# Tiles of rows j and j+3 of one batch, numerator products over 128 rows, and a new written order, in a linear attention kernel with a mixture of adapters behind it

## The chip, the core and the metric

The kernel runs on one core of a Trainium2 chip. The metric is the time of the device for one execution, in microseconds (us). One execution of the kernel before was also taken by the hardware profiler; its rows are what the profile shows. Engines: TensorE (PE in the profile, PEld for its weight loads), VectorE (DVE), ScalarE (ACT), GpSimd (POOL), SyncE (SP, which issues every DMA here, one queue, in program order).

## The reference

Two parts, one behind the other. For each of 8 batches and 8 heads, with 576 rows of 64 columns:

```python
theta = np.pi / 2.0 * pos / S
def phi(x, c, s):
    r = np.maximum(x, 0.0)
    return np.concatenate([r * c, r * s], axis=-1)
q_p, k_p = phi(q, cos_w, sin_w), phi(k, cos_w, sin_w)
kv  = np.einsum('bhsf,bhsd->bhfd', k_p, v)
z   = np.sum(k_p, axis=2)
num = np.einsum('bhsf,bhfd->bhsd', q_p, kv)
den = np.einsum('bhsf,bhf->bhs', q_p, z)[..., None] + 1e-06
x   = num / den                      # then laid out as (8*576, 8*64)
logits = x @ w_gate                  # 8 experts, the best 2 kept, softmax weights w
out = x + sum over the 2 of  w * (x @ A[e]) @ B[e]        # rank 16
```

Inputs q, k and v are 28.3 MB in float32, the output is 9.4 MB.

## The kernel before

Rows of a batch are laid out as row 9p+j, with p in 0..63 and j in 0..8: half a partition axis holds the 64 values of p. Two heads share the partitions on loading (`load`, L381: `"b (g hp) (p j) d -> (hp p) (b g) (j d)"`), so a load has 128 partitions. K and Q come in units: batches 0 to 3 alone (1.18 MB each), batches 4 and 5 together and 6 and 7 together (2.36 MB each). V comes by batch.

Work on a unit, by the names that the written order uses:

- `LK0`, `LV0`, `LQ0`: a load. `st8.0`: store 0 of the group of tiles that ends with tile 8.
- `cK0.1`, `cQ0.1` (`e_cast`, L429): a pass over three values of j, 768 columns for a single batch or 1536 for two, float32 to bfloat16. For K it is also the relu (ScalarE at L436 or VectorE at L438); for Q it is a cast alone (L301, L303, L305), the relu of Q comes later.
- `phiK0.4`, `phiQ0.4` (`e_phi`): the second half of the features, the first half times tan (L309 on ScalarE, L312 on VectorE and GpSimd), 256 or 512 columns. `vs0.4`: V times cos into the `vb` tile, with the same two lines.
- `kv0.1` (L496): 24 products that add up K'V of a batch; `ke0` copies the result out of PSUM.
- `tq7` (L603): 8 transposes that bring a tile's Q features onto the partitions. `eq6` (L620, L622): copies two tiles out of PSUM, with Q's relu, into a `qt` tile.
- `nd7` (`e_nd`, L637): numerators and denominators of a tile. A tile is 128 rows in two halves of 64. For each of 8 heads and each half there is one product with 64 stationary columns (L645), which writes the half's 64 partitions of PSUM, and four more products add the epsilon (L652).
- `rd6`, `nx6` (L671, L676): reciprocal and multiplication, two tiles together, into an `x` tile.
- `tx7`, `ex6` (L696): transposes of x and their copy. `za7` (L721): products with the adapters' A and the gate. `mx`, `nt`, `d`, `ge`, `sg`, `w`, `zg`: the choice of two experts and their weights, for a group of tiles. `tz`, `ez` (L782): transpose of the weighted z and its copy. `dx7` (L806, L808): x plus the adapters' product. `eo6`: copy of the output of one or two tiles into an `o` tile (six of them; three lie in the first K buffer, once K4 has been read).

There are 36 tiles in groups. For batches 0 to 3 a tile pairs rows j and j+5 of one batch (j in 0..3), and row 4 is paired with that of another batch; batches 4 to 7 pair the same row of two batches. Groups are of two or three tiles, and one at the end: 15 groups.

Nothing decides the order at run time. The string `ORDER` lists every operation with its engine (`=V` VectorE, `=S` ScalarE, `=G` GpSimd) and its buffer (`@2`), and `replay` (L127) emits them in that order. Each engine takes its own instructions strictly in the listed order, and waits for what the instruction reads and for its buffer. `fill=14@0` stands for 14 matmuls of no use to the result (L832). SP's order of loads is `LQ0 LK0 LV0 LQ1 LV1 LK1 LK2 LQ2 LV2 ldw LQ3 LK3 LV3 LK4 LV4 LV5 LQ4 LK6 LV7 LV6`, two stores (`st1.0 st1.1`), `LQ6`, and then the other stores.

Of the kernel before, what the change touches and what calls it, by code (L numbers as in the profile page):

```python
# [72 lines left out]
LK3@3 phiQ0.8=G kv0.2 cQ1.2=G@3 tq3 ke0=S@0 cQ1.0=S@5 nd0@2 cQ1.1=G@4 nd1 fill=7@6 phiQ1.2=S
phiQ1.0=V phiQ1.5=G eq2=S@1 LV3@0 vs1.0=V@1 phiQ1.8=G rd0@1 vs1.4=G nx0@1 phiQ1.6=G sig vs1.7=G
tq4@4 phiQ1.1=G nd2@0 vs1.8=G tx0@6 cK1.0=V@2 phiQ1.7=S nd3 vs1.5=G cK1.1=V@3 tx1 fill=7@7
phiK1.2=S vs1.6=G vs1.2=S cK1.2=V@4 phiK1.5=G rd2@0 LK4@0 phiK1.7=S phiK1.3=G nx2@0 vs1.1=S
phiQ1.3=G cK2.2=S@1 vs1.3=G phiK1.4=V tq6@0 phiK1.1=G cK2.1=S@0 LV4@1 phiK1.8=V tq5 phiK1.0=V
eq4=S@1 phiQ1.4=V kv1.0@2 phiK1.6=V cK2.0=V@5 kv1.1 kv1.2 phiK2.6=V cQ2.0=G@0 tq7 ke1=V@3
ex0=S@1 tx2@7 tx3 cQ2.1=G@2 phiK2.1=V nd4@2 nd5 fill=6@6 phiQ2.2=S phiK2.7=G phiK2.5=V
phiK2.0=S rd4@0 phiK2.2=S nx4@2 vs2.0=G@2 phiQ2.0=S vs2.1=G vs2.2=S phiK2.4=V vs2.7=G vs2.4=S  # L80
eq6=V@1 kv2.0@2 vs2.5=S phiQ2.5=G tq8@4 phiQ2.1=S vs2.3=G tq9 aw phiK2.8=S phiK2.3=G tx4@6 tx5
vs2.6=S vs2.8=G ex2=V@0 za0@0 cQ2.2=S@5 LV5@2 kv2.1 eq8=V@0 kv2.2 LQ4@0 za2@1 cQ3.2=G@3 ke2=S@1
za1 za3 mx2@0 ex4=S@1 mx0@1 nd8@2 mx1 phiQ3.6=G mx3 nd9 fill=8@7 ge1 nt1=V nt3=G ge3 phiQ2.8=G
d1 phiQ2.7=V sg1 cQ3.1=G@4 cQ3.0=S@1 d3 rd8@2 w1=V phiQ2.3=S nx8@3 phiQ3.1=G cK3.0=S@1 zg1
cK3.1=S@0 nd6@2 phiK3.1=G phiQ3.7=V nd7 phiK3.0=G phiQ3.2=V tz1@0 sg3 tq12@6 w3=G ez1=S@1 rd6@1
phiK3.2=G nx6@4 phiQ3.0=S za4@0 za5 vs3.0=G@0 cK3.2=S@2 vs3.2=G mx4@2 tq14@4 vs3.7=S mx5 LK6@2
phiK3.6=G phiQ3.5=V dx0@2 nt5=V phiK3.7=S phiK3.8=G d5 dx1 zg3 vs3.8=G ge5 eo0=S@0 tx8@1
phiK3.3=V tq15 vs3.5=V vs3.4=G eq14=V@1 vs3.1=S tz3@3 tq13 phiK3.5=G vs3.3=S tx6@2 vs3.6=G tx7
ez3=S@0 phiK3.4=V kv3.0@4 phiQ2.6=G eq12=V@0 sg5 ex6=S@0 kv3.1 phiQ2.4=G kv3.2 phiQ3.3=G tx9
w5=V ke3=S@0 dx2@2 zg5 ex8=V@1 cK4.0=S@2 tz5@0 nd14@4 nd15 ez5=V@1 dx4@0 rd14@1 nx14@1 dx5  # L90
phiK4.1=G dx3 eo4=S@1 phiQ3.8=G eo2=V@2 tq10@4 phiK4.2=G tq11 cK4.1=S@4 za9@6 tx14@0 eq10=V@1
tx15 za6@7 za7 phiK4.5=G za8 ex14=S@1 mx6@0 nd10@2 mx7 cK4.2=V@0 nd11 fill=7@1 phiK4.0=S rd10@2
mx8 vs4.0=S@1,2 vs4.7=G nt8=V vs4.8=S vs4.2=G nx10@2 phiK4.7=S vs4.5=G vs4.1=V tx10@5 phiQ3.4=S
d8 kv5.0@0 mx9@1 sg8 phiK4.3=V vs4.6=S vs4.4=G tx11 ge8 phiK4.8=V tq16@2 phiK4.6=S vs4.3=G tq17
ex10=V@0 phiK4.4=G eq16=S@1 LV7@1 w8=V za10 kv4.0@4 LV6@0 mx10 kv4.1 zg8 nt10=G cQ4.1=G@2 kv5.1
st1.0 cQ4.0=V@0 kv4.2 tz8@7 st1.1 ke4=S@3 kv5.2 cQ4.2=G@4 LQ6@2 nd12@2 nd13 st5.1 d10 ez8=V@1
sg10 ke5=S@2 ge10 rd12@0 nx12@0 phiQ4.1=S dx6@0 phiQ4.3=G dx7 phiQ4.0=G dx8@7 w10=V eo6=S@3
phiQ4.4=G zg10 eo8=V phiQ4.5=S tz10@7 st8.0 cK6.1=S@2 nd16@2 ez10=V@0 nd17 cK6.0=V@0 tq18@0
za15@6 cK6.2=S@4 rd16@0 tq19 nx16@4 za11@7 eq18=S@0 phiK6.8=G phiQ4.2=V tx16@2 tx17 mx15@1
tq20@4 ex16=V@0 phiK6.6=G tq21 mx11@2 tx12@3 phiQ4.6=G eq20=V@1 za16 tx13 za17 dx9@0 ex12=S@0  # L100
dx10 mx16 mx17 ge17 nt17=G eo9=S@4 phiK6.2=G za12 d17 nd18@2 mx12 nt12=V nd19 phiK6.7=G d12
sg17 st10.0 ge12 tq22@0 sg12 rd18@1 vs6.0=G@0,1 nx18@3 tq23 st3.1 w12=G eq22=S@0 st10.1 w17=G
phiK6.3=G zg12 nd20@2 zg17 tz12@7 phiK6.0=G nd21 ez12=V@0 dx11@6 vs6.8=S rd20@2 phiQ4.7=G
tz17@0 nx20@2 dx12 vs6.2=G ez17=S@1 za13@1 za14 eo11=S@5 tx18@0 vs6.3=G mx13@0 dx15@2 mx14 ge14
tq24@4 nt14=V phiK6.4=G d14 vs6.1=V tq25 sg14 vs6.5=S cQ6.0=G@0 dx16 eq24=V@1 tx20@6 eo15=S@0
tx21 dx17@7 tx19 w14=V vs6.4=G zg14 nd22@2 ex18=S@1 ex20=V@0 nd23 vs6.7=G tz14@1 rd22@0
ez14=S@0 phiQ6.2=G nx22@4 eo17=S dx13@0 dx14 phiK6.5=V nd24@2 eo13=S@4 phiK6.1=V nd25 phiQ4.8=V
kv6.0@6 vs6.6=V phiQ6.0=S st14.1 kv6.1 rd24@0 nx24@0 za18@1 cQ6.2=S@2 st17.0 za19 kv6.2 st12.1
# [759 lines left out]
```

## Time and profile before

| | us |
|---|---|
| median of 3 runs | 124.34 (124.27 to 124.65) |
| profiled execution | 124.38 |
| its span, first to last instruction | 122.6 |
| TensorE busy | 98.9 (81% of the span) |
| VectorE busy | 88.6 (72%) |
| ScalarE busy | 87.4 (71%) |
| GpSimd busy | 61.4 (50%) |

DMA moved 38.59 MB. "Busy" counts the time of instructions, with their pipeline latency: single matmuls are given with 0.2 to 0.4 us where the next one starts 0.02 to 0.2 us later, so a step's cost on TensorE is read from the distance of starts, or from the chain of waits, which counts each stretch once. A row of the timeline gives start, duration, engine, line, operation, output and input; in brackets stand the idle time ahead of it and what ended that.

### The profile page before, as it was taken

The numbers are of one execution on the slowest core, as the hardware profiler recorded it, in microseconds if no ns is written. First come the engines' busy times: TensorE is split into PE (matmuls) and PEld (weight loads), VectorE is DVE, ScalarE is ACT, GpSimd is POOL, SyncE is SP. The second block draws the span as 40 slices with busy tenths as digits, with TensorE's granted clock in tenths as the row PEclk, the third lists the DMA queues.
The fourth block names the chain that finished last, engine by engine and source line by source line (L and its number), as shares of the span: only waits on it lengthen the run. The fifth ranks groups of instructions, "written<-read, shape, count | busy, mean of one in ns | idle before, by whom it ended". The sixth has DMA issues, their size and how long they took to land.

```text
span 122.6 us, 4766 instructions
## 1 busy us (share of the span) xinstructions
PE 98.9 (81%) x2048; PEld 71.9 (59%) x2048; DVE 88.6 (72%) x225; ACT 87.4 (71%) x130; POOL 61.4 (50%) x114
## 2 busy tenths in 40 slices
PE   4969795859698889998875697999998979999720
PEld 1334563457484768676745567776897866874300
DVE  1008625597988888999496879899689978878700
ACT  5049489389967996989865996897984685767720
POOL 3045999366659696539497189846390010011000
PEclk9999999999999999999999999999999999999997
DMA  2999999999999999999999999960698100997992
GB/s 56 404 396 392 390 396 388 392 388 351 349 393 391 391 387 386 390 389 388 388 390 388 392 405 406 398 274 21 170 233 246 55 0 15 397 274 269 349 410 94
DMA packets 16532, 38.59 MB, mean 315 GB/s; under 512 B 1920, under 2 KB 1920, under 8 KB 16512
## 3 DMA queue, kind: packets, MB, share of 16 engines
q1 hardware_dynamic: 16512, 38.29, 86.4%
q8 instruction: 16, 0.26, 1.0%
q14 instruction: 4, 0.03, 0.1%
HBM read 28.85 MB, written 9.44 MB: 312 GB/s over the span
## 4 chain that ended last, share of the span: by engine, by line
DMA 42%; PE 21%; DVE 17%; SPq 11%; issue 2%; ACT 1%; POOL 0%; DVEq 0%
DMA k<-in_k_dram 28%; DMA v<-in_v_dram 14%; SPq L384 11%; DVE x L676 7%; PE psum L603 5%; PE psum L721 4%; PE psum L696 3%; PE psum L645 3%; PE psum L808 2%; PE psum L806 2%; DVE qt L622 2%; DVE zg L766 1%; DVE rd L671 1%; PE psum L782 1%; ACT xt L301 1%
## 5 line engine op out<-in xcount | busy, mean ns | idle before, releaser
L603 PE MATMUL psum<-ident,qp 128*128 128x128 bf16 x288 | 20.3, 219 | 5.7 <-DVE x L676 3.7
L676 DVE TENSOR_TENSOR x<-psum,rd 128x1024 bf16<-128x1024 f32 (+1 forms) x19 | 22.2, 1168 | 0.7
L603 PEld LDWEIGHTS <-qp 128*128 128x128 bf16 x288 | 17.0, 98 | 8.6 <-issue 4.7
L312 POOL TENSOR_SCALAR kp<-kp,tanw 128x256 bf16<-128x256 bf16 (+1 forms) x24 | 14.3, 601 | 11.6 <-ACT kp L436 9.5
L312 POOL TENSOR_SCALAR vb<-v,cosw 128x256 bf16<-128x256 f32 (+1 forms) x32 | 17.8, 567 | 3.9 <-DMA v<-in_v_dram 3.8
L303 POOL CAST qp<-q 128x768 bf16<-128x768 f32 (+1 forms) x11 | 12.2, 1125 | 14.8 <-DMA q<-in_q_dram 9.0
L832 PE MATMUL psum<-ident 128*128 128x512 bf16 x68 | 17.6, 409 | 1.9 <-POOL ident masks.py:199 1.8
L645 PE MATMUL psum<-kv,qt 128*64 128x65 bf16 x576 | 14.1, 197 | 2.8 <-DVE x L676 2.6
L645 PEld LDWEIGHTS <-qt 128*64 128x64 bf16 x576 | 12.4, 111 | 6.0 <-issue 3.6
L620 ACT ACTIVATE qt<-psum 128x2048 bf16<-128x2048 bf16 (+1 forms) x8 | 14.1, 1758 | 2.5 <-PE psum L603 1.6
L312 POOL TENSOR_SCALAR qp<-qp,tanw 128x256 bf16<-128x256 bf16 (+1 forms) x26 | 14.5, 564 | 0.3
L806 PE MATMUL psum<-x,ident 128*128 128x512 bf16 x36 | 13.7, 379 | 0.7 <-ACT kv L301 0.6
L436 ACT ACTIVATE kp<-k 128x768 bf16<-128x768 f32 (+1 forms) x10 | 10.7, 1094 | 5.0 <-DMA k<-in_k_dram 5.0
L622 DVE TENSOR_SCALAR qt<-psum 128x2048 bf16<-128x2048 bf16 (+1 forms) x11 | 12.9, 1170 | 1.8 <-PE psum L603 1.5
L808 PE MATMUL psum<-Bb,zt 128*128 128x512 bf16 x36 | 13.7, 379 | 0.1
L696 PE MATMUL psum<-ident,x 128*128 128x128 bf16 x144 | 12.4, 221 | 1.5 <-DVE x L676 1.5
L721 PE MATMUL psum<-AW,xt 128*128 128x136 bf16 x144 | 12.7, 223 | 1.2 <-DVE xt L305 0.3
L496 PE MATMUL psum<-vb,kp 64*128 64x65 bf16 x576 | 11.5, 190 | 1.2 <-POOL vb L312 1.1
L832 PEld LDWEIGHTS <-ident 128*128 128x128 bf16 x68 | 6.6, 104 | 9.7 <-issue 2.2
L696 PEld LDWEIGHTS <-x 128*128 128x128 bf16 x144 | 9.6, 114 | 4.0 <-DVE x L676 2.7
L438 DVE TENSOR_SCALAR kp<-k 128x768 bf16<-128x768 f32 (+1 forms) x8 | 5.0, 654 | 9.4 <-DMA k<-in_k_dram 9.4
L496 PEld LDWEIGHTS <-kp 64*128 64x128 bf16 x576 | 9.8, 94 | 3.1 <-issue 1.1
(56 smaller groups left out, 166.6 us busy)
## 6 DMA issues: line engine op xcount, KB each, us to landing
v<-in_v_dram SPq DMA_DIRECT2D x8, 1152.0 KB, 15.2
q<-in_q_dram SPq DMA_DIRECT2D x4, 1152.0 KB, 10.5
k<-in_k_dram SPq DMA_DIRECT2D x4, 1152.0 KB, 13.6
k<-in_k_dram SPq DMA_DIRECT2D x2, 2304.0 KB, 18.8
q<-in_q_dram SPq DMA_DIRECT2D x2, 2304.0 KB, 17.8
out_dram<-k SPq DMA_DIRECT2D x10, 256.0 KB, 5.1
out_dram<-o SPq DMA_DIRECT2D x9, 256.0 KB, 5.5
out_dram<-o SPq DMA_DIRECT2D x3, 768.0 KB, 5.1
```

Source lines behind the costliest of these rows:

```text
L312: eng.tensor_scalar(out=o_ap, in0=i_ap, scalar1=by, scalar2=0.0, op0=ALU.mult, op1=ALU.add)
L496: nc.tensor.matmul(out=psum[:, s + hp, h2 * W:(h2 + 1) * W], lhsT=kp[hp * 64:hp * 64 + 64, bi * H2 + h2, :], rhs=vb_t[hp * 64:hp * 64 + 64 ...
L603: nc.tensor.transpose(out=o_ap[:, hi, h2, :], in_=qv[:, bi * H2 + h2, :], identity=ident)
L620: nc.scalar.activation(o_ap, i_ap, AF.Relu)
L622: nc.vector.tensor_scalar(out=o_ap, in0=i_ap, scalar1=0.0, scalar2=None, op0=ALU.max)
L645: nc.tensor.matmul(out=psum[hi * 64:hi * 64 + 64, s + g, x * W:(x + 1) * W], lhsT=qt[:, qi, hi, h2, hp * 64:hp * 64 + 64], rhs=kv_t[KV[b][ ...
L676: nc.vector.tensor_tensor(out=x_t[Y["x"].slot][:, 0:n].rearrange("p n (g i d) -> p (n g) i d", g=2, i=4), in0=f()[:, :, :, 0:D], in1=r().t ...
L696: nc.tensor.transpose(out=bank16(s, 1024)[:, i * 512 + c * 128:i * 512 + (c + 1) * 128], in_=xv[:, c, :], identity=ident)
L721: nc.tensor.matmul(out=psum[:, s, i * ZW:(i + 1) * ZW], lhsT=xt_t[Z["xt"].slot][:, zi, c, :], rhs=AW[:, c, :], start=(c == 0 and i == 0), ...
L806: nc.tensor.matmul(out=psum[:, s, :], lhsT=ident, rhs=x_t[Y["x"].slot][:, yi, :], start=True, stop=False)
L808: nc.tensor.matmul(out=psum[:, s, :], lhsT=zt_t[Gd["zt"].slot][:, i, :], rhs=Bb, start=False, stop=True)
L832: nc.tensor.matmul(out=psum[:, s, :], lhsT=ident, rhs=warm, start=True, stop=True, skip_group_check=True)
```

## The change

1. Tiles. For every batch, tiles 0 to 2 of it hold rows j and j+3 of that batch (j = 0, 1, 2; stored as two stores of 64 partitions with three rows each), and rows 6 to 8 are paired with those of the other batch of a pair. 24 of 36 tiles are then of one batch. All groups have three tiles, but the last two (two and one): 13 groups instead of 15, 21 stores instead of 25.
2. In a tile of one batch both halves multiply the same K'V, so one product with 128 stationary columns does both: 8 products and 2 for the epsilon instead of 16 and 4. `qt` is laid out so that a head's two halves lie side by side, which changes where `tq` writes in PSUM, and not its count. A small tile `epsx` holds the epsilon of both halves.
3. The relu pass of K may run on GpSimd too, as a `tensor_scalar` with max, float32 to bfloat16. The new order puts 7 of the 18 there (five of 768 columns, two of 1536), 7 on ScalarE and 4 on VectorE; before it was 10 and 8.
4. `ORDER` is a new one: other order, engines and buffers throughout. Loads: `LK0 LQ0 LK1 LV0 LV1 LQ1 LK2 ldw LV2 LQ2 LK3 LQ3 LV3 LV5 LV4 LK4 LQ4 LK6 LV6 LV7 LQ6`, and then all stores. Matmuls of `fill`: 42 at the start, then 1, 3 and 3 (before 14, 19, 7, 7, 6, 8, 7).

```diff
-                    nc.vector.tensor_scalar(out=o_ap, in0=i_ap, scalar1=0.0, scalar2=None,
-                                            op0=ALU.max)
+                    eng = nc.vector if e == "DVE" else nc.gpsimd
+                    eng.tensor_scalar(out=o_ap, in0=i_ap, scalar1=0.0, scalar2=None, op0=ALU.max)
...
+    for b in range(0, B, 2):
+        for c in (b, b + 1):
+            rows = out[c * S:(c + 1) * S].rearrange("(p j) c -> p j c", j=NJ)
+            group([[(c, j), (c, j + 3)] for j in range(3)],
+                  [(64 * y, 64 * y + 64, 0, 3, rows[:, 3 * y:3 * y + 3, :]) for y in range(2)])
+        rows = out[b * S:(b + 2) * S].rearrange("(p j) c -> p j c", j=NJ)
+        j0 = 6
+        for gn in ((2, 1) if b == B - 2 else (3,)):
+            group([[(b, j), (b + 1, j)] for j in range(j0, j0 + gn)],
+                  [(0, 128, 0, gn, rows[:, j0:j0 + gn, :])])
+            j0 += gn
...
-                        nc.tensor.transpose(out=o_ap[:, hi, h2, :],
+                        nc.tensor.transpose(out=o_ap[:, h2, :, hi, :],
...
+                one = hv[0][0] == hv[1][0]
                 for g in range(2):
                     for x in range(4):
                         h = 4 * g + x
                         h2, hp = h // 2, h % 2
+                        if one:
+                            nc.tensor.matmul(
+                                out=psum[:, s + g, x * W:(x + 1) * W],
+                                lhsT=qt[:, qi, h2, hp, :, :],
+                                rhs=kv_t[KV[hv[0][0]]["kv"].slot][:, hp, h2, :],
+                                start=(x == 0), stop=False, skip_group_check=True)
+                            continue
                         for hi, (b, j) in enumerate(hv):
                             nc.tensor.matmul(
                                 out=psum[hi * 64:hi * 64 + 64, s + g, x * W:(x + 1) * W],
-                                lhsT=qt[:, qi, hi, h2, hp * 64:hp * 64 + 64],
+                                lhsT=qt[:, qi, h2, hp, hi, :],
                                 rhs=kv_t[KV[b]["kv"].slot][:, hp, h2, :],
                                 start=(x == 0), stop=False, skip_group_check=True)
```

The places of the new order that the prediction speaks of:

```
... cK2.0=G@0 ... cK2.1=G@5 ... phiQ1.7=G phiK2.5=G ... phiK2.7=G ... phiK2.0=G ... phiK2.3=G ... phiK2.2=G ...
vs2.8=G ... vs2.4=G phiK2.4=G ... vs2.1=G ... cQ2.0=G@1 ... phiQ2.0=G ... vs2.7=G ... vs2.5=G ... LV5@2
...
tq18@4 rd16@1 phiQ4.5=G nx16@3 za13 tq19 cK6.1=S@4 cK6.2=G@0 eq18=V@0 tx16@7 za14 tq20@0
cK6.0=S@2 phiQ4.8=G tx17 mx13 nd18@2 ... nd19 ... tq21 rd18@0 ex16=S@0 ... za15@7 ... tq22@4 ... tq23 ... za16
...
cQ6.0=G@4 ... cQ6.1=G@0 ... tq26@2 phiQ6.3=V ... tq27 cQ6.2=G@2 ... kv7.0@0
```

More of the change, by code (lines that the diff above doesn't have):

```diff
@@ L73 @@
[L73 to L108, printed above, removed]
```

130 lines of the change are left out of this document (75 added, 55 removed).

## The prediction

> **What bounds the kernel now.** I read four views in this order: the page's DMA line, the busy times by stretch, the chain of waits, and the timeline of single engines where the chain turns. First the DMA rate in 40 slices of 3.07 us, and three stretches cut where the chain turns.
>
> ```profile
> span 122.6 us, 4766 instructions
> ...
> GB/s 56 404 396 392 390 396 388 392 388 351 349 393 391 391 387 386 390 389 388 388 390 388 392 405 406 398 274 21 170 233 246 55 0 15 397 274 269 349 410 94
> ...
> core 0: us, PE busy (x) PEld busy (x) DVE busy (x) ACT busy (x) POOL busy (x), PEclk, DMA share, GB/s
> 0.00:66.90 66.90, 53.77 (x1138) 37.47 (x1139) 46.61 (x114) 48.57 (x78) 43.63 (x83) 1.00 1.02 372
> 66.90:110.00 43.10, 38.77 (x855) 31.55 (x853) 36.52 (x93) 32.94 (x42) 17.37 (x29) 1.00 0.69 237
> 110.00:122.60 12.60, 6.37 (x61) 2.85 (x59) 5.45 (x20) 5.84 (x11) 0.43 (x2) 0.95 0.74 278
> ```
>
> Loads stream at about 390 GB/s until slice 26, that is until 80 us, and nothing on the engines can bring them sooner. In the first 66.9 us no engine is full (VectorE 46.6, ScalarE 48.6). Then TensorE is busy 38.8 of 43.1 us and VectorE 36.5. Where it turns stands in the chain of waits (start, length, what):
>
> ```profile
> 0.73 0.45 SPq L384
> ...
> 32.48 34.38 DMA k<-in_k_dram x2
> ...
> 66.88 0.96 DVE kp L438
> ...
> 68.04 1.24 DVE x L676
> ...
> 69.33 0.64 PE psum L696 x8
> ...
> 116.80 0.40 PE psum L808
> ...
> 117.22 0.58 ACT k L301
> ```
>
> The load of K6 lands at 66.9. VectorE waits for it with `cK6.0`, so `nx16` comes late and TensorE has nothing to do until `tx16` at 69.33. From there TensorE works off what is left, to `dx35` at 117.20. Behind that lie 5.4 us (last copy, last store, end of the program), and 1.78 us between the span and the time of the profiled execution (124.38, 0.04 above the median). So the kernel is: wait for K6, then work off a backlog. Two things move its end: when K6 lands, and how much TensorE has left then.
>
> **The change, part by part.** *Loads.* The timelines give landings by the instruction that waited for each:
>
> ```profile
> 6.40 0.83 ACT L301 CAST qp<-q 128x768 bf16<-128x768 f32 x1 [3.97 <-DMA q<-in_q_dram]
> 31.87 1.39 POOL L312 TENSOR_SCALAR vb<-v,cosw 128x256 bf16<-128x256 f32 x3 [0.98 <-DMA v<-in_v_dram]
> 42.78 0.97 POOL L312 TENSOR_SCALAR vb<-v,cosw 128x256 bf16<-128x256 f32 x2 [0.48 <-DMA v<-in_v_dram]
> 66.94 2.86 ACT L436 ACTIVATE kp<-k 128x1536 bf16<-128x1536 f32 x2 [1.52 <-DMA k<-in_k_dram]
> 81.27 1.46 POOL L303 CAST qp<-q 128x1536 bf16<-128x1536 f32 x1 [1.99 <-DMA q<-in_q_dram]
> 60.18 3.63 SPq L824 DMA_DIRECT2D out_dram<-o  x2
> ...
> out_dram<-o SPq DMA_DIRECT2D x9, 256.0 KB, 5.5
> ```
>
> Before, the first load lands at 6.40 and V2, the ninth, at 31.87: (31.87 - 6.40) / 8 = 3.18 us for 1.18 MB. In both orders 12 such units and the adapter weights stand up to V3 (42.8), and 20 units up to K6. So K6 lands at 66.9 in the new order too, if SP never waits for a buffer. Q6 comes sooner: two stores of 256 KB stood ahead of it, 0.52 MB at 390 GB/s is 1.3 us, so 79.9.
>
> The place where SP could wait is `LV5`, which now stands right behind `LV3`: its buffer is V2's, so all nine `vs2` have to be done, and behind LV5 in SP's row stand LV4, LK4, LQ4, LK6 and all else. LV5 has to be issued some 2.6 us ahead of V3's landing (the first load was issued at 0.73, took 3.1 us to stream and landed at 6.40): by 40.2. The last of the nine is `vs2.5` on GpSimd, behind 15 others from `cK2.0` on. Prices on GpSimd, and of the other passes that come up below (mean ns after the comma):
>
> ```profile
> L312 POOL TENSOR_SCALAR vb<-v,cosw 128x256 bf16<-128x256 f32 x22 | 10.7, 498 | 2.0 <-DMA v<-in_v_dram 2.0
> L312 POOL TENSOR_SCALAR vb<-v,cosw 128x512 bf16<-128x512 f32 x10 | 7.1, 720 | 1.8 <-DMA v<-in_v_dram 1.8
> L303 POOL CAST qp<-q 128x768 bf16<-128x768 f32 x7 | 5.7, 834 | 8.4 <-DMA q<-in_q_dram 7.0 <-PE psum L721 1.4
> L312 POOL TENSOR_SCALAR kp<-kp,tanw 128x256 bf16<-128x256 bf16 x13 | 6.7, 522 | 5.3 <-ACT kp L436 3.2 <-DVE kp L438 2.1
> L312 DVE TENSOR_SCALAR qp<-qp,tanw 128x512 bf16<-128x512 bf16 x3 | 1.5, 506 | 0.0
> L301 ACT COPY xt<-psum 128x1024 bf16<-128x1024 bf16 x9 | 9.1, 1012 | 1.8 <-PE psum L721 1.4 <-PE psum L696 0.2
> ```
>
> The relu of K on GpSimd isn't in the trace. Below it can't be cheaper than the cast of the same columns (0.83); the `tensor_scalar` from float32 grows by 0.22 per 256 columns, which gives 0.94; the upper end is twice that, 1.9, if max costs a second pass. I take 0.94, the nearest row. K2, the seventh unit, lands at 6.40 + 6 x 3.18 = 25.5. Two relus, 13 passes of 0.50 and the cast of Q2: 25.5 + 1.9 + 6.5 + 0.8 = 34.7. But that cast waits for Q2 (tenth behind the weights, 33.2), and three passes follow: 33.2 + 0.83 + 1.5 = 35.5. That is 4.7 us of cover; with the dear relu it is 36.6, still 3.6. So this part costs nothing as long as no other engine is over 4 us late there.
>
> *Up to K6.* By counts from the two orders, VectorE has to do more ahead of its K6 work than before: one `nx` and `rd`, one `eq`, seven `phiQ`, three `vs`, against three relus of K, one cast, one `eo` and one group's choice less, some 2 us net. ScalarE and GpSimd change by under 2 us, and TensorE has 19 useless matmuls less in all. Against 20 us in which VectorE was not busy there (66.9 - 46.6), that fits.
>
> *The backlog.* The new order lays `cK6` on ScalarE (two) and GpSimd (one), so VectorE no longer waits, and TensorE can go on past K6's landing, through `tq23` and `za15`, to `za16`. This waits for `ex16`, which stands behind two relus on ScalarE: 66.9 + 2.86 + 1.01 = 70.8. Steps on TensorE, from the chain:
>
> ```profile
> 69.96 0.89 PE psum L603 x16
> 70.86 0.22 PE psum L696 x4
> 71.08 0.24 PE psum L721 x4
> ...
> 76.40 0.37 PE psum L645 x16
> 76.78 0.04 PE psum L652 x4
> ...
> 88.87 0.47 PE psum L496 x24
> ...
> 109.22 0.17 PE psum L782 x3
> ...
> 110.28 0.22 PE psum L806
> 110.49 0.22 PE psum L808
> ```
>
> So `tq` is 0.445 (half of 0.89), `tx` 0.22, `za` 0.24, `nd` 0.41, a `kv` 0.47, `tz` 0.17, `dx` 0.44. Before, from `tx16` on: 16 tq, 22 tx, 23 za, 18 nd, 6 kv, 10 tz, 27 dx, which is 41.3 us. They took 117.20 - 69.33 = 47.9, a factor of 1.16 for waits.
>
> The new `nd` of one batch: 8 products of 65 columns over 128 stationary columns, not in the trace. Below, 65 columns at the rate of the 512-column product, 0.22 x 65 / 512 = 0.028; above, the 128-column transpose, 0.445 / 8 = 0.056. With two epsilon products of 0.01 a tile is 0.24 to 0.47. I take 0.33, nearer to the lower end, because the pairs of half width (0.37 / 8 = 0.046) already load 128 stationary columns between them.
> [...]
>
> After, from `za16` on: 12 tq, 18 tx, 20 za, 10 nd at 0.33 and 6 at 0.41, 6 kv, 9 tz, 24 dx, which is 34.8 us. Of the 6.5 us less, 0.8 is nd; the rest is work that the new order has behind it by then (three tiles' `dx` and `za`, four `tq`, one group less). At the same factor: 34.8 x 1.16 = 40.3.
>
> One new wait: all three `cQ6` are on GpSimd. Q6 lands at 79.9, two casts of 1.46 and `phiQ6.3` (0.51 on VectorE) bring `tq27` to 83.3. TensorE would be there after 9.4 us of steps, 70.8 + 9.4 x 1.16 = 81.7. So it waits 1.6, and `kv7`, `nd24` and all behind it in its row wait too. The first stores now start behind Q6. With six output buffers the first copy that needs one back is `eo18`, some 6 us of TensorE steps behind `tq27`, near 90; the stores ahead of it (1.5 MB, 4 us) are out by 85. So nothing for these.
>
> *The sum.* 70.8 + 40.3 + 1.6 + 5.4 = 118.1 of span, + 1.78 = **119.9 us**, 4.4 under the median.
>
> **The rivals.** *The factor doesn't hold.* A shorter backlog may leave the chains between engines as they are (`rd`, `nx`, `tx`, `ex`, `za`), so that TensorE idles more. VectorE's backlog shrinks too (one relu, one `nx` and `rd`, three copies, one choice, about 5 us), which speaks against it. For it speaks that 1.16 was reached where TensorE was busy 38.77 of 43.10 us, so that its waits were few already, and that a chain from one tile's products to its output has the same length as before. At 1.24 the backlog takes 43.2: 122.8 us.
>
> *The load queue runs dry (slower).* If `vs2.5` ends after 40.2, SP idles, and each us of it moves K4, Q4, K6, Q6 and the whole backlog by one. It decides from 40.2 + 4.4 = 44.6 on. For it: the nine `vs2` are spread over three in-order engines, with waits for TensorE (`ex4`, `eq6`) between them, and GpSimd has been given relus ahead of them. Against it: 4.7 us of cover. Were it at 47, the time would be 126.7.
>
> *TensorE's clock.* The 42 useless matmuls end at 1.83 + 3.6 + 34 x 0.22 = 12.9, and `tq0` waits for K1's relu on GpSimd (K1 lands at 12.8) and four passes on ScalarE, near 15.7, a pause of 2.8 us, with only seven more of them later. The trace shows what a cold start costs:
>
> ```profile
> 1.83 3.58 PE L832 MATMUL psum<-ident 128*128 128x512 bf16 x8 [1.83 <-POOL ident masks.py:199]
> ...
> 8.34 1.90 PE L832 MATMUL psum<-ident 128*128 128x512 bf16 x8
> ```
>
> Eight took 3.58 us at the start and 1.90 later, with the granted clock at 1.00 in both. A pause that brings this back costs 1.7 us each time, in a stretch where TensorE isn't full; should it reach the backlog once, 121.6.
> [...] No run here shows such a pause.
>
> *It doesn't do what it says:* the joined products gain nothing (0.47 instead of 0.33). That is 10 x 0.14 x 1.16 = 1.6 us: 121.5, still faster.
>
> **How the numbers follow.** Forecast 0.54, with a range of its own from 117.5 (no wait at Q6, nd at its lower end) to 121.8 (nd at its upper end). Factor 0.16, clock 0.05, joined products of no use 0.04, load queue dry 0.21, of which small bubbles end below or near the time before. The range takes in all but the longer bubbles: 117.2 to 124.8. A measurement tells a change of 0.3% (0.4 us) from none. Faster by more: 0.54 + 0.05 + 0.04, 0.10 of the factor's 0.16 and 0.04 of the dry queue's 0.21: 0.77. Within: 0.04 and 0.02 of the same two, 0.06. Slower: 0.02 and 0.15, 0.17.
>
> **What would show it.** K6's relus start at 66.9 (dry queue: later, with a dip in the DMA rate near 40 us). TensorE's first step that waits for ScalarE is `za16` near 71. The products over 128 columns start 0.03 to 0.056 apart. `tq27` waits for GpSimd or VectorE near 82. `dx35` ends near 112.7. The prediction is wrong if K6 lands late, or if TensorE waits over 8 us in all between 71 and 112.

## The result, and the profile after

The changed kernel takes 130.78 us (median of four, 129.39 to 130.98) against 124.31 for the kernel before beside it: 1.049 times as long, with a 95% interval of 1.043 to 1.056. The forecast was 119.9, with a range up to 124.8: faster was forecast, and it became slower. Medians, ranges and ratios are those of the faster executions of a kernel, within 1.5% of its fastest, and slower ones are left out unless the text lists all. The profiled execution took 129.39 us; its span of 127.6 stands against the 118.1 that the prediction added up.

From the page of the changed kernel, the span, the granted clock and the DMA rate in 40 slices of 3.19 us:

```profile
span 127.6 us, 4227 instructions
...
PEclk9999968999999859999955899999999999999965
...
GB/s 64 408 394 391 392 391 393 317 388 394 391 390 391 389 391 391 389 393 391 389 396 389 392 382 94 0 5 61 243 314 250 235 322 242 208 234 229 248 311 90
```

The loads stream at 390 GB/s to the end of slice 23, at 76.6 us, no later than before. Slice 7 (slices count from 0) dips to 317, and no slice is empty: the load queue did not run dry. So it wasn't data that was late. Behind the loads next to nothing moves for some 10 us, and then stores run at 208 to 322 GB/s to the end.

Busy times in four stretches, cut at K6's landing, at `za16` and at the end of `dx35`:

```profile
core 0: us, PE busy (x) PEld busy (x) DVE busy (x) ACT busy (x) POOL busy (x), PEclk, DMA share, GB/s
0.00:66.90 66.90, 49.45 (x913) 36.00 (x915) 48.68 (x108) 44.90 (x76) 51.76 (x78) 0.93 1.02 373
66.90:81.70 14.80, 10.99 (x200) 8.79 (x195) 13.12 (x19) 9.74 (x12) 10.60 (x12) 0.85 0.74 274
81.70:119.40 37.70, 36.45 (x688) 27.70 (x685) 31.30 (x86) 30.30 (x45) 14.39 (x26) 1.00 0.76 208
119.40:127.60 8.20, 0.00 (x0) 0.00 (x0) 0.00 (x0) 0.54 (x1) 0.00 (x0) 0.68 0.67 208
```

From 81.7 to 119.4 TensorE is busy 36.45 of 37.7 us. That stretch is healthy and shorter than forecast. The loss lies ahead of it: by 66.9 us TensorE had started 913 matmuls of 1789 (51%) where it had started 1138 of 2048 before (56%), and GpSimd had worked 51.8 us in place of 43.6. Two groups by shape show what GpSimd did, and two of VectorE's what happened beside it (count, busy us, mean ns of one):

```profile
L440 POOL TENSOR_SCALAR kp<-k 128x768 bf16<-128x768 f32 x5 | 10.8, 2156 | 2.2 <-DMA k<-in_k_dram 2.2
...
L440 POOL TENSOR_SCALAR kp<-k 128x1536 bf16<-128x1536 f32 x2 | 8.2, 4092 | 0.5 <-DMA k<-in_k_dram 0.5
L311 DVE TENSOR_SCALAR kp<-kp,tanw 128x512 bf16<-128x512 bf16 x6 | 5.3, 942 | 0.0
...
L311 DVE TENSOR_SCALAR qp<-qp,tanw 128x512 bf16<-128x512 bf16 x3 | 4.9, 1669 | 0.0
```

A relu of K on GpSimd takes 2.16 us for 768 columns and 4.09 for 1536, where the prediction took 0.94. And VectorE's passes over 512 columns of `qp` take 1.67 us each, where they took 0.51. The timelines of VectorE and GpSimd, laid side by side at three places, tell why (start, length):

```profile
54.80 4.08 POOL L440 TENSOR_SCALAR kp<-k 128x1536 bf16<-128x1536 f32 x1 [0.50 <-DMA k<-in_k_dram]
...
56.58 2.58 DVE L311 TENSOR_SCALAR vb<-v,cosw 128x512 bf16<-128x512 f32 x1
...
60.81 5.01 DVE L311 TENSOR_SCALAR kp<-kp,tanw 128x512 bf16<-128x512 bf16 x5
...
62.69 2.98 POOL L302 CAST qp<-q 128x1536 bf16<-128x1536 f32 x2
...
70.57 4.58 DVE L311 TENSOR_SCALAR qp<-qp,tanw 128x512 bf16<-128x512 bf16 x2
...
70.90 4.11 POOL L440 TENSOR_SCALAR kp<-k 128x1536 bf16<-128x1536 f32 x1
```

Add start and length. GpSimd's relu ends at 58.88, VectorE's one pass at 59.16. The relu `cK6.2` ends at 75.01, VectorE's two passes at 75.15. The two casts end at 65.67, the five passes, which take 2.60 us where no cast comes (the kernel with the relus on VectorE, below), at 65.82. So it looks as if VectorE's pass stops until GpSimd's long instruction is done, and its in-order row behind it; a kernel of single instructions tests it below. On TensorE that reads:

```profile
75.87 0.61 PE L592 MATMUL psum<-ident,qp 128*128 128x128 bf16 x8 [2.93 <-DVE xt L304]
...
81.72 0.40 PE L725 MATMUL psum<-AW,xt 128*128 128x136 bf16 x4
...
118.93 0.39 PE L812 MATMUL psum<-Bb,zt 128*128 128x512 bf16 x1
```

TensorE idles 2.93 us for a copy of VectorE that stands behind the held passes. `za16` comes at 81.72 in place of 70.8, `dx35` ends at 119.32, and the span ends 8.3 us later, where the prediction took 5.4.

### The profile page after: what moved, and what is told of

Same layout as the page of the kernel before. It is cut to its first block, busy times and chain, and to the rows that moved or that the text cites. A ratio compares the mean times of both kernels' runs of the same rounds, so it can differ in the third digit from the quotient of the medians.

```text
span 127.6 us, 4227 instructions
## 1 busy us (share of the span) xinstructions
PE 96.9 (76%) x1789; PEld 72.5 (57%) x1789; DVE 93.1 (73%) x212; ACT 85.5 (67%) x132; POOL 76.7 (60%) x115
## 4 chain that ended last, share of the span: by engine, by line
PE 34%; DVE 24%; DMA 12%; POOL 10%; issue 6%; SPq 4%; ACT 4%; POOLq 0%; DVEq 0%
DMA q<-in_q_dram 12%; PE psum L592 7%; PE psum L812 5%; PE psum L810 5%; DVE x L680 5%; DVE qt L611 5%; PE psum L700 4%; DVE kp L311 4%; PE psum L635 4%; SPq L385 4%; PE psum L725 4%; POOL kp L440 3%; ACT qt L609 3%; DVE qp L311 2%; PE psum L495 2%
## 5 line engine op out<-in xcount | busy, mean ns | idle before, releaser
L592 PE MATMUL psum<-ident,qp 128*128 128x128 bf16 x288 | 21.6, 223 | 9.9 <-ACT qp L308 3.7
L440 POOL TENSOR_SCALAR kp<-k 128x768 bf16<-128x768 f32 (+1 forms) x7 | 18.9, 2709 | 2.7 <-DMA k<-in_k_dram 2.7
L611 DVE TENSOR_SCALAR qt<-psum 128x2048 bf16<-128x2048 bf16 x12 | 14.6, 1217 | 3.2 <-PE psum L592 3.1
L495 PEld LDWEIGHTS <-kp 64*128 64x128 bf16 x576 | 10.9, 100 | 7.9 <-issue 3.7
L311 POOL TENSOR_SCALAR vb<-v,cosw 128x256 bf16<-128x256 f32 (+1 forms) x27 | 15.0, 566 | 0.0
L838 PE MATMUL psum<-ident 128*128 128x512 bf16 (+1 forms) x49 | 13.1, 425 | 1.8 <-POOL ident masks.py:199 1.8
L609 ACT ACTIVATE qt<-psum 128x2048 bf16<-128x2048 bf16 (+1 forms) x7 | 11.4, 1634 | 4.4 <-PE psum L592 3.5
L300 ACT COPY xt<-psum 128x1024 bf16<-128x1024 bf16 (+1 forms) x10 | 9.6, 968 | 4.5 <-PE psum L700 4.5
L311 DVE TENSOR_SCALAR qp<-qp,tanw 128x256 bf16<-128x256 bf16 (+1 forms) x15 | 9.8, 670 | 3.1 <-ACT qp L300 2.4
L300 ACT COPY k<-psum 128x1024 f32<-128x1024 f32 (+1 forms) x12 | 9.3, 801 | 3.8 <-POOL qp L311 2.2
L749 POOL TENSOR_TENSOR ss<-m 128x3 f32<-128x3 f32 x8 | 1.6, 197 | 16.7 <-DVE m L736 15.4
```

Source lines behind the costliest of these rows:

```text
L300: nc.scalar.copy(o_ap, i_ap)
L311: eng.tensor_scalar(out=o_ap, in0=i_ap, scalar1=by, scalar2=0.0, op0=ALU.mult, op1=ALU.add)
L440: eng.tensor_scalar(out=o_ap, in0=i_ap, scalar1=0.0, scalar2=None, op0=ALU.max)
L495: nc.tensor.matmul(out=psum[:, s + hp, h2 * W:(h2 + 1) * W], lhsT=kp[hp * 64:hp * 64 + 64, bi * H2 + h2, :], rhs=vb_t[hp * 64:hp * 64 + 64 ...
L592: nc.tensor.transpose(out=o_ap[:, h2, :, hi, :], in_=qv[:, bi * H2 + h2, :], identity=ident)
L609: nc.scalar.activation(o_ap, i_ap, AF.Relu)
```

## The experiments

Executions of one kernel with the new order still lie up to 1.8 us apart, so a difference under 1 us is not read from the medians. The kernel before, run beside each group of experiments, took 124.25 to 124.75 us.

**The relus taken off GpSimd.** Three kernels, of which the first is

```diff
-cK0.0=G@0 ... cK1.1=G@2 ... cK2.0=G@0 ... cK2.1=G@5 ... cK3.0=G@2 ... cK4.0=G@0 ... cK6.2=G@0
+cK0.0=V@0 ... cK1.1=V@2 ... cK2.0=V@0 ... cK2.1=V@5 ... cK3.0=V@2 ... cK4.0=V@0 ... cK6.2=V@0
```

> The changed kernel with the seven relu passes of K that it gives to GpSimd (cK0.0, cK1.1, cK2.0, cK2.1, cK3.0, cK4.0, cK6.2) on VectorE, at the same places of the order. Theory (the relu on GpSimd takes 2.16 us for 768 columns and 4.09 for 1536 where 0.94 was assumed, and passes of VectorE that start meanwhile wait for its end, so that the work around K6 comes some 6 us late): without it the time falls to 118 to 122 us, za16 starts near 71 to 73 and no pass of VectorE from SBUF over 512 columns takes more than 2 us beside a GpSimd relu. Rival A (the new order itself is late, its waits lie in the rows of the engines whatever the relu costs): the time stays at 127 to 131, and TensorE idles around 60 to 77 us as before. Rival B (TensorE's granted clock, which falls to 0.72 at 60 to 70 us because only 65 useless matmuls stand in place of 84, slows the end): the time stays above 126 with the granted clock at 0.93 as in the changed kernel.

The second leaves them on GpSimd, but as casts; the relu of these seven is left out:

```diff
+                    if e == "DVE":
+                        nc.vector.tensor_scalar(out=o_ap, in0=i_ap, scalar1=0.0, scalar2=None, op0=ALU.max)
+                    else:
+                        nc.gpsimd.tensor_copy(o_ap, i_ap)
```

> The changed kernel with the seven GpSimd passes of K as plain casts to bf16: the relu is left out of these seven passes, all else is as it was, on the same engine and at the same place. Theory (the form of the instruction is dear, not the work given to GpSimd): casts cost 0.88 and 1.49 us in place of 2.16 and 4.09, that is 5 x 1.28 + 2 x 2.6 = 11.6 us less on GpSimd, and the time falls to 118 to 122 us. Rival A (the new order is late by itself): 127 to 131. Rival C (any pass of 768 or 1536 columns on GpSimd holds VectorE up, whatever its form): VectorE's passes of 512 columns beside these casts still take over 2 us and the time falls by less than half of what it falls when the passes go to VectorE.

The third gives the order of before the same seven relus on GpSimd (`=S` and `=V` made `=G` at `cK0.0`, `cK1.1`, `cK2.0`, `cK2.1`, `cK3.0`, `cK4.0`, `cK6.2`).

> The kernel before, with its own order and tiles, and the same seven relu passes of K given to GpSimd at the places where they stood: this part of the change alone. Theory (the relu's price and VectorE's waits behind it make the loss): slower than before by 4 to 12 us, GpSimd passes L440 at 2.1 to 2.2 us (768 columns) and near 4.1 (1536). Rival A (the new order makes the loss): within 2 us of before, 124 to 126.

| kernel | us (range) | ratio to before |
|---|---|---|
| changed | 130.78 (129.39 to 130.98) | 1.049 (1.043 to 1.056) |
| relus on VectorE | 121.69 (121.16 to 122.54) | 0.979 (0.973 to 0.985) |
| casts on GpSimd | 121.21 (121.06 to 121.48) | 0.975 (0.972 to 0.978) |
| order of before, relus on GpSimd | 132.54 (132.11 to 133.22) | 1.067 (1.062 to 1.072) |

The relus on GpSimd cost the old order 8.3 us, and the new order gains 9.1 when they go to VectorE. This settles the first question: the seven GpSimd relus make the loss, and the new order by itself is faster than before. The casts show that it isn't the work given to GpSimd but this instruction. The granted clock isn't the cause either: the kernel with casts ran its profiled execution at a mean of 0.949 and still took 121.5, and the old order with the relus took 132.3 at 0.958. From the timelines of the kernel with the relus on VectorE, ScalarE first, then TensorE:

```profile
66.83 2.86 ACT L437 ACTIVATE kp<-k 128x1536 bf16<-128x1536 f32 x2 [0.69 <-DMA k<-in_k_dram]
...
73.84 0.40 PE L725 MATMUL psum<-AW,xt 128*128 128x136 bf16 x4
...
111.04 0.39 PE L812 MATMUL psum<-Bb,zt 128*128 128x512 bf16 x1
```

K6's relus start with the landing at 66.8, as forecast (in the changed kernel 73.63). `za16` comes at 73.84, `dx35` ends at 111.43.

**What the relu costs by itself.** A kernel of prices:

```python
ts(out=dst("onemax"), in0=i_ap, scalar1=0.0, scalar2=None, op0=ALU.max)                        # L58
ts(out=dst("twomax"), in0=i_ap, scalar1=0.0, scalar2=0.0, op0=ALU.max, op1=ALU.add)            # L59
ts(out=dst("onemul"), in0=i_ap, scalar1=1.0, scalar2=None, op0=ALU.mult)                       # L60
ts(out=dst("twomul"), in0=i_ap, scalar1=1.0, scalar2=0.0, op0=ALU.mult, op1=ALU.add)           # L61
nc.gpsimd.tensor_copy(dst("cast"), i_ap)                                                       # L65
```

> Prices by themselves; the kernel computes none of the reference's output. GpSimd runs, twice each, over 768 columns from float32 to bf16: max with an immediate as one operation, max followed by an add in one instruction, one multiplication, multiplication followed by an add, the same with the scalar read from a column, a cast, a max over 768 columns in one stretch and a max from bf16. Then VectorE runs passes of 512 columns (tensor_scalar from bf16, copy from PSUM, tensor_scalar from float32, tensor_tensor of bf16) three times alone and eight times beside GpSimd's max and cast. Theory: max costs near 2.16 us in every form of one operation and the multiplication with an add near 0.94; whether the form with two operations makes max cheap is open (if so, it takes 0.9 to 1.1). VectorE's passes from SBUF that start during a GpSimd pass end with it (up to 2.1 us in place of 0.3 to 0.5), while its copies from PSUM keep their time. Rival C: all forms of 768 columns cost about the same on GpSimd, and 2.16 us in the changed kernel came from contention with VectorE. Rival D: VectorE's copies from PSUM are held up as well, which would make it a matter of waits and not of the SBUF side.

Its groups of GpSimd, and rows of VectorE's and GpSimd's timelines: the pass over 512 columns from bf16 (L72) and from float32 (L75), alone near 44 us and beside one of GpSimd's relus of 768 columns near 68 us:

```profile
L59 POOL TENSOR_SCALAR ptwomax<-src 128x768 bf16<-128x768 f32 x2 | 5.6, 2778 | 0.0
...
L60 POOL TENSOR_SCALAR ponemul<-src 128x768 bf16<-128x768 f32 x2 | 4.3, 2137 | 0.0
...
L58 POOL TENSOR_SCALAR ponemax<-src 128x768 bf16<-128x768 f32 x2 | 4.2, 2124 | 5.8 <-DMA src<-in_q_dram 5.8
...
L61 POOL TENSOR_SCALAR ptwomul<-src 128x768 bf16<-128x768 f32 x2 | 1.7, 832 | 0.0
L65 POOL CAST pcast<-src 128x768 bf16<-128x768 f32 x2 | 1.6, 822 | 0.0
```

```profile
43.67 0.35 DVE L72 TENSOR_SCALAR dbfo<-dbf,one 128x512 bf16<-128x512 bf16 x1
...
44.53 0.48 DVE L75 TENSOR_SCALAR df32o<-df,one 128x512 bf16<-128x512 f32 x1
...
67.97 2.12 POOL L87 TENSOR_SCALAR busy<-src 128x768 bf16<-128x768 f32 x1
...
68.32 0.62 DVE L72 TENSOR_SCALAR dbfo<-dbf,one 128x512 bf16<-128x512 bf16 x1
...
69.46 0.91 DVE L75 TENSOR_SCALAR df32o<-df,one 128x512 bf16<-128x512 f32 x1
```

Two forms are fast, the cast and multiply-then-add, at 0.82 and 0.83 us. One multiplication alone takes 2.14, as long as max. So the prediction read a price off the one fast `tensor_scalar` in the trace, the multiply-and-add of `vs`, and gave it to another operation. The rival (all forms alike, contention with VectorE) is out, since these ran with VectorE idle. VectorE's passes beside relus of 768 columns lost at most 0.43 us, so the theory holds only in part for this length. The relu runs from 67.97 to 70.09. The float32 pass, started at 69.46, ends at 70.37, behind the relu; the bf16 pass, started at 68.32, ends at 68.94, in the middle of it.

**What holds VectorE.** One GpSimd instruction of 1536 columns at a time, and behind its start on VectorE a PSUM copy and two passes.

> Prices by themselves; the kernel computes none of the reference's output. First three other forms of the relu on GpSimd over 768 columns (the relu instruction, multiply by 1 followed by max, add of 0 followed by max). Then one GpSimd instruction over 1536 columns at a time (none, max, cast, multiply and add) and behind its start on VectorE a copy from PSUM and two passes: of the kernel's phi form (8 runs of 64 in bf16), of one row of 512, of two inputs, or from PSUM again. Theory (a pass of VectorE from SBUF with one input that starts during a GpSimd instruction ends with it): the phi form takes 0.34 to 0.5 us alone and 2.5 to 4 us beside max (4.1 us), up to 1.3 us beside the cast (1.5 us); copies from PSUM keep 0.69 us. Rival (it is slowed, not stopped, as the first probe's passes were, by 0.1 to 0.45 us): no pass over 1 us. For the relu forms: open; a form under 1.1 us would make the change's relus cheap.

From the timelines, in order of time: two phi passes of VectorE alone, GpSimd's max, the passes beside it, two passes beside a cast, and three copies from PSUM beside another max:

```profile
22.31 0.73 DVE L69 TENSOR_SCALAR dphi<-dphi,tan 128x512 bf16<-128x512 bf16 x2
...
23.39 4.08 POOL L60 TENSOR_SCALAR gmax<-srce 128x1536 bf16<-128x1536 f32 x1
...
24.13 3.87 DVE L69 TENSOR_SCALAR dphi<-dphi,tan 128x512 bf16<-128x512 bf16 x2
...
29.02 1.24 DVE L69 TENSOR_SCALAR dphi<-dphi,tan 128x512 bf16<-128x512 bf16 x2
...
58.38 2.13 DVE L79 CAST dps<-acc 128x512 bf16<-128x512 f32 x3
```

Max runs to 27.47; two passes that take 0.73 alone last from 24.13 to 28.00, while three copies from PSUM take 2.13 us, with nothing beside them (at 55.77) and beside max. Nothing in the program makes the passes wait, and of these two forms only the one that reads SBUF is held. The pass is held to the end beside 1536 columns (3.87 against 0.73), and not beside the relu of 768, which let a pass end in its middle (68.94, above). The other forms of the relu, at 2.13 to 2.79 us, were no cheaper.

The changed kernel's own trace shows that the hold isn't a matter of 1536 columns. A pass of 256 columns on VectorE, free and then beside the second of two casts of 768 columns on GpSimd:

```profile
11.67 0.28 DVE L311 TENSOR_SCALAR qp<-qp,tanw 128x256 bf16<-128x256 bf16 x1 [0.72 <-POOL qp L302]
...
40.09 1.91 POOL L302 CAST qp<-q 128x768 bf16<-128x768 f32 x2
...
41.33 0.76 DVE L311 TENSOR_SCALAR qp<-qp,tanw 128x256 bf16<-128x256 bf16 x1
```

The casts end at 42.00, the pass at 42.09. Three of the five passes near 61 us, 0.33 us free, took 0.68 to 0.78 beside GpSimd's passes of 512 columns, and the most that a relu of 768 cost one instruction was 0.62 (a cast on VectorE at 29.47). So short instructions held VectorE too, for up to 0.62 us here; the long `cK6.2` held a pass for 3.64 (4.15 in place of 0.51).

**Price or hold?** In one kernel each GpSimd relu is cut into three instructions, one for each j; in two others only the two long relus, or only the five short ones, go to VectorE.

```diff
-                    eng.tensor_scalar(out=o_ap, in0=i_ap, scalar1=0.0, scalar2=None, op0=ALU.max)
+                        for y in range(3):
+                            nc.gpsimd.tensor_scalar(out=o_ap[:, :, y, :], in0=i_ap[:, :, y, :], scalar1=0.0,
+                                                    scalar2=None, op0=ALU.max)
```

> The changed kernel with each of its seven GpSimd relus cut into three instructions, one a row j (256 or 512 columns each); GpSimd has the same work and some 14 fixed costs more. It tells how much of the loss is GpSimd's own time and how much is VectorE held up for the length of one GpSimd instruction. If the holding up counts: VectorE's longest passes of 512 columns fall from 4.15 us to 1.6 or less and the time falls by 2 us or more, to 125 to 129. If only GpSimd's time counts: 130 to 133 us.

> The changed kernel with only the two relus of 1536 columns (cK4.0, cK6.2) on VectorE; the five of 768 columns stay on GpSimd at 2.16 us each. Theory A (an instruction of 1536 columns on GpSimd holds VectorE up to its end, one of 768 doesn't, so the two late relus make most of the loss): 122.5 to 125 us, of the 8.7 us between the changed kernel and the one with all seven on VectorE at least two thirds are gone. Theory B (the price alone counts, and the five early ones carry 5 x 1.2 = 6 us of the 11.6): 126 to 129 us, with K4 and K5's work late by 50 us already.

> The changed kernel with only the five relus of 768 columns (cK0.0, cK1.1, cK2.0, cK2.1, cK3.0) on VectorE; the two of 1536 columns stay on GpSimd at 4.09 us each. Theory A: 127 to 131 us, VectorE's passes beside the two still take 2.5 to 4.2 us and K6's relus on ScalarE start later than 70 us. Theory B: 123 to 126 us.

In thirds: 123.02, 125.41, 126.24 and 126.36 us, each under the 129.39 to 130.98 of the whole relus, though GpSimd is busy 79.2 us in place of 76.7. So the length of one instruction counts, for 3 to 8 us. Two long relus on VectorE: 124.09 (123.50 to 125.31; all ten executions 123.50 to 126.96). Five short ones: 125.30 in one execution, 129.11 to 129.41 in the three others.

Of the 9.1 us between the changed kernel and the one with all seven on VectorE, the long relus alone bring back 6.7, or 5.1 by the median of all ten executions; the short ones alone bring 5.5 in the one execution and some 1.5 in the others. The long ones weigh more, as theory A had it, but the parts don't add up to 9.1 either way, and how they split stays open. What is left in all three blurs it: in their profiled executions (126.24, 125.53 and 129.30 us) VectorE's five passes near 59 us still took 4.9 to 5.1 us behind Q4's two casts. And a hold isn't all that a long relu costs: with the five short ones on VectorE, VectorE stands idle for 3.02 us, to 58.91, for the result of the long relu of K4.

**Casts in thirds, too.** For Q's casts of 1536 columns the same cut, with the seven relus on VectorE:

> The kernel with the seven relus on VectorE, with GpSimd's five casts of 1536 columns cut into three of 512. Theory (an instruction of 1536 columns on GpSimd holds VectorE's passes up to its end, one of 512 or 768 doesn't): no pass of VectorE of 512 columns takes more than 0.7 us, and the time is the same or up to 1 us lower than with whole casts, 121 to 122.3; VectorE's phi passes of K4 near 58 us no longer change from run to run. Rival (three more fixed costs on GpSimd cost more than the holding up): 122.5 to 124 us.

121.31 us (121.20 to 122.93), the same as with whole casts. The passes of K4 took 0.55 us in the mean and up to 0.79, over the 0.7 expected, beside GpSimd's passes of 512 columns. Inconclusive for the time: where the relus are cheap, VectorE's passes were mostly done before the casts came.

**The joined products.** `one = False` in the kernel with the relus on VectorE:

> The kernel with the seven relus on VectorE, with the 24 joined tiles computed as before the change: 16 products over 64 columns and four epsilon products in place of 8 over 128 columns and two. Prediction's term (the joined tile takes 0.30 to 0.33 us, the pair form 0.41): slower than the joined form by 0.5 to 2 us, 122.5 to 124, with these tiles at 0.34 to 0.41 us. Rival (pairs of 64 columns run side by side, so joining gains nothing): within 0.3 us of the joined form or faster, tiles at 0.30 us or less.

127.87 us (126.73 to 128.05), 6.2 above the joined form, far more than either side expected. In the profiled execution:

```profile
58.97 5.01 DVE L311 TENSOR_SCALAR kp<-kp,tanw 128x512 bf16<-128x512 bf16 x5
...
71.13 2.85 ACT L437 ACTIVATE kp<-k 128x1536 bf16<-128x1536 f32 x2
...
116.03 0.39 PE L812 MATMUL psum<-Bb,zt 128*128 128x512 bf16 x1
```

From K6's first relu to the end of `dx35` it takes 116.42 - 71.13 = 45.3 us, against 111.43 - 66.83 = 44.6 with joined products: 0.7 more, the prediction's 0.8. The other 4.3 us are lost ahead of K6: VectorE comes to its five passes 1.4 us later (58.97 against 57.53), so they meet Q4's casts on GpSimd at 60.86 and take 5.0 us in place of 2.6. That reading of one execution each makes a small delay large by the hold; it was not tried by itself.

**The end.** With the relus on VectorE the span still ends 8.4 us behind the last product. Five kernels ask why. One store in place of each pair of half stores:

```diff
-                  [(64 * y, 64 * y + 64, 0, 3, rows[:, 3 * y:3 * y + 3, :]) for y in range(2)])
+                  [(0, 128, 0, 3, rows[:, 0:6, :].rearrange("p (y j) c -> y p j c", y=2))])
```

> The kernel with the seven relus on VectorE, and each pair of stores that covers partitions 0 to 63 and 64 to 127 of one group made one store over all 128 partitions, at the place of the earlier of the two (13 stores in place of 21, the same 9.44 MB). In the run with the relus on VectorE the last product ended at 111.4 us but the span at 119.8, 8.4 us later where the kernel before has 5.4; from 80 us on the DMA engines were 87 to 99% busy at 220 to 285 GB/s, against 390 GB/s for loads. Theory (stores from one half of the partitions move at about two thirds of the rate, and with all stores behind the last load they are late at the end): the rate rises to 350 or more where stores are waiting, the end behind the last product falls to 5.4 to 6 us and the time to 119 to 120. Rival (the rate is that of any store, or the tail is the chain of the last tile): within 0.5 us of the run with the relus on VectorE, 121.2 to 122.6, with the tail at 8 us.

210.13 us, and its page shows how the stores ran (DMA engines' mean busy share in tenths, and the rate):

```profile
DMA  6999999999999980114111114111123111114110
GB/s 207 397 391 394 344 386 390 389 391 390 392 393 389 391 321 33 55 57 186 52 54 54 52 61 180 57 53 53 54 103 136 52 54 53 53 54 184 54 52 38
```

The stores run at 53 GB/s with the sixteen DMA engines busy at 0.1 to 0.2 on the mean, some two of them (0.13 of the sixteen from 100 to 104 us). That the outer dimension of two is the cause is the author's guess, and no other run tried it. It tells nothing of the half stores. Next, second halves on another queue, and full stores with the rows put elsewhere:

> The kernel with the seven relus on VectorE, and six of the sixteen stores that cover one half of the partitions (the second halves of the groups that end with tiles 5, 14, 20, 23, 29 and 32) issued from GpSimd's queue in place of SP's. In the run with the relus on VectorE the DMA engines were 95 to 100% busy at 200 to 250 GB/s while such stores ran and moved 390 to 410 where a store over all partitions ran. Theory (a half's stores have half the way into SBUF; two halves at once share it out): the rate rises above 300 GB/s where both queues have work, the end behind the last product falls from 8.4 towards 5.4 us, and the time to 119.5 to 121. Rival (the rate of a store over 64 partitions doesn't depend on what runs beside it): 121.5 to 123 us, the rate stays at 200 to 250.

> The kernel with the seven relus on VectorE, with the two stores of each one-batch group changed from two halves of the partitions (three rows each) to all 128 partitions (two rows, then one): as many stores and bytes, at the same places of the order, but the rows are put at other places of the output. Theory (half the partitions, two thirds of the rate or less): no stretch of full DMA engines under 300 GB/s, dx35 as before at 111 and the end behind it at 5.4 to 6 us: 118.5 to 120 us. Rival (the stores' number or place in the order makes the tail): 121.2 to 123 us, with the last stores issued near 113.6 as in that run.

Two queues: 121.57 us (121.31 to 121.82), 258 GB/s from 100 to 104 us (in an execution of 127.5) where one queue gave 210; no gain in time. Full stores: 118.65 (117.55 to 118.81). In stretches of 4 us (the last two columns are the DMA engines' share and the rate), first the kernel with the relus on VectorE while half stores run:

```profile
100.00:104.00 4.00, 4.00 (x67) 2.98 (x64) 3.42 (x12) 2.66 (x5) 0.42 (x2) 1.00 1.00 210
```

then the kernel before while it stores full partitions:

```profile
116.00:120.00 4.00, 0.83 (x3) 0.21 (x3) 0.41 (x2) 1.29 (x2) 0.00 (x0) 1.00 1.00 407
```

and the last product of the kernel with full stores, whose span is 115.8 us:

```profile
110.42 0.39 PE L812 MATMUL psum<-Bb,zt 128*128 128x512 bf16 x1
```

210 GB/s against 407 with the DMA engines full in both, and the end behind the last product falls from 8.4 to 115.8 - 110.8 = 5.0 us. The new tiles put 16 of 21 stores on half of the partitions: 6.3 MB at 210 GB/s and 3.1 MB at 400 are 38 us, in the kernel with the relus on VectorE from the first store at 80 to 118. The prediction did not weigh this.

> The kernel with the seven relus on VectorE and GpSimd's casts of 1536 columns in thirds, with the two stores of the first group (tiles 0 to 2) moved ahead of the load of Q6, to see whether the stores behind the loads bound the end. From 80 us to the last store 8.65 MB are then left in place of 9.44. Theory (the stores' own stream ends the kernel): 0.8 MB at 210 GB/s is 3.7 us less behind the loads against 2 to 3.7 us by which Q6 lands later; as TensorE had no wait over 1 us for Q6, the end comes 1 to 2.5 us earlier: 119 to 121.3 us. Rival (Q6's landing decides): 122.5 to 125 us, TensorE waits for Q6 over 2 us near 83 to 90.

123.23 us (122.77 to 123.66) against 121.31 with the casts in thirds alone: the rival's range, though hardly by its mechanism, for TensorE waited 0.84 us for Q6's features and never over 1 us from 70 us on. The last product ends 2.05 us later (112.82 against 110.77), and most of that is not explained. The end behind it stayed at 8.2 us. So it isn't the sum of the stream that bounds the end (the DMA engines are at 0.77 to 0.82 from 104 to 112 us in the kernel with the relus on VectorE), but the last half stores: an earlier start brings nothing, another shape does. Last, tiles of batches 4 to 7 back to pairs of two batches with full stores, with the relus on VectorE and the casts in thirds:

```diff
+        if q_of[b][0] == q_of[b + 1][0]:
+            j0 = 0
+        else:
+            for c in (b, b + 1):
...
+        for gn in (3,) * ((6 - j0) // 3) + ((2, 1) if b == B - 2 else (3,)):
```

> The kernel with the seven relus on VectorE and GpSimd's casts in thirds, with the tiles 18 to 23 and 27 to 32 (batches 4 to 7, loaded two at a time) as pairs of one row of two batches, as before the change: 16 products of half width in place of 8 in these twelve tiles, and four stores over all partitions in place of eight over one half. Theory (stores over one half, at some 210 GB/s against 400, end the kernel late): 3.1 MB move in 8 us in place of 15, the end behind the last product falls from 8.4 to 5.5 us or less; against it twelve tiles cost 0.05 us more each on TensorE, 0.6 us in all: 118.5 to 120.5 us, the best of the kernels that compute the whole. Rival (the dearer tiles on TensorE, seen to cost 5.8 us when all 24 were undone, take back the gain): 121.5 to 125 us, dx35 ends at 113 us or later.

118.20 us (118.10 to 119.41; all six executions 118.10 to 121.25), 0.951 (0.946 to 0.957) of the time before: the best of those that compute the whole.

The stretch in which its last stores run, and its last product:

```profile
112.00:116.00 4.00, 1.59 (x6) 0.35 (x6) 0.70 (x4) 1.85 (x4) 0.00 (x0) 1.00 0.97 391
```

```profile
113.38 0.39 PE L819 MATMUL psum<-Bb,zt 128*128 128x512 bf16 x1
```

The last stores run at 391 GB/s and the span ends 119.1 - 113.8 = 5.3 us behind the last product, in an execution of 121.0.

## Why the prediction was wrong, step by step

- *Loads.* Right. With the relus on VectorE, K6's relu starts with its landing at 66.83 (66.9 forecast) and Q6's cast at 80.34 (79.9). In the changed kernel `LV5` was issued at 37.47, inside the cover of 40.2. The rival of a dry queue did not come.
- *The relu of K on GpSimd* (0.94 us, upper end 1.9). This is the step that failed. It takes 2.16 us for 768 columns, above the upper bound: none of the forms of max that were tried (2.12 to 2.86 us) is as fast as the cast (0.82) and the multiply-add (0.83). The two of 1536 columns, `cK4.0` and `cK6.2`, stand in the sum at nothing; they take 4.09 us each. And the cost was looked for in the load queue alone ("that is 4.7 us of cover"), not on the engine beside it.
- *Up to K6, "that fits".* Wrong. GpSimd's work there grew by 8.1 us (43.6 to 51.8) and not by "under 2", and VectorE's passes between SBUF tiles were held beside its long instructions (one beside `cK4.0` for 2.58 us, five beside Q4's casts 5.01 in place of 2.60). Without the relus on GpSimd it did fit, as K6's relus start with the landing, but barely: even with casts in their place VectorE was busy 9.93 of 10 us from 50 to 60 us, although the average over 66.9 us showed room.
- *`za16` at 70.8.* 81.72. With the relu out of the way 73.48 (casts) and 73.84 (VectorE): some 8 us of the 10.9 are the relu's. Of the other 3, 2.1 are waits of TensorE for VectorE's `x` and `qt` (0.45, 0.68 and 0.96 us with the relus on VectorE), not for ScalarE as the prediction had it.
- *The backlog, 40.3 + 1.6.* 119.32 - 81.72 = 37.6, and 37.6 with the relus on VectorE as well. The factor was 37.6 / 34.8 = 1.08, not 1.16 and not the rival's 1.24, and `tq27` did not wait for Q6. This term was 4.3 too dear.
- *The joined products.* Right in size: starts 82.28 and 82.58, so 0.30 a tile (0.33 taken), and 0.7 us in the backlog. The rival that joining gains nothing fell.
- *The end, 5.4.* 8.3. Stores were priced at the loads' rate ("1.5 MB, 4 us"), and half stores moved at half of it (210 GB/s against 390).
- *The sum.* 118.1 + 10.9 - 4.3 + 2.9 = 127.6, the span. The backlog's error of 4.3 hid part of the loss, which was luck. The forecast's own range comes out as 117.3 to 121.5 by its terms, and not 117.5 to 121.8; nothing hangs on it.
- *The clock rival.* The granted clock did fall: it was 0.50 from 16.8 to 20.0 us, behind TensorE's wait of 3.71 us to 17.28, where transposes started 0.105 us apart in place of 0.055, and 0.50 again from 65.0 to 71.2, with TensorE waiting to 65.97 (2.24 us) and busy from there on. Through the 2.93 us to 75.87 it stayed at 1.00. But executions at 0.949 and 0.958 took 121.5 and 132.3. What a pause costs, 1.7 us in the rival, was not tried by itself. (There are 49 useless matmuls in place of 68; the expectation that speaks of 65 and 84 has them wrong, the difference right.)

The slower rival given, a dry load queue at 126.7, came nearest in time, 4 us under the result, and was wrong in mechanism.

## What to carry to other kernels

Price an operation by its own row, or by a small kernel that runs it alone: on GpSimd two `tensor_scalar` forms over the same columns lay 2.6 times apart (2.14 us and 0.83). Before giving GpSimd a long instruction, look at what VectorE does between SBUF tiles meanwhile (two passes took 3.87 us here in place of 0.73), and cut the instruction if that can't move (the relus in thirds: 123.02 to 126.36 us in place of 129.39 to 130.98). When tiles are rearranged, look at how many partitions each store covers (210 GB/s here over 64, 407 over 128), and price stores by the rows of such stores.
